# Lightweight convolution into a gated FFN: two of VectorE's 18 convolution group tasks move to GpSimd, and TensorE's convolution blocks become three of 80 windows and one of 40

## The chip, the core and the metric

The kernel runs on one core of one Trainium2 chip. The metric is the device time of one execution in microseconds (us), the median of three runs. The engines are named as the profile names them: PE is TensorE, DVE is VectorE, ACT is ScalarE, POOL is GpSimd, SP is the queue that issues most of the DMAs.

## What is computed

The input `x` is 8 sequences of 3904 rows with 192 channels. Each row becomes a weighted sum of itself and the six rows before it in its sequence (zeros ahead of a sequence's first row). The seven weights are a softmax and are shared by the 24 channels of a head. The result goes through a gated feed-forward network without a nonlinearity. Cut to what matters:

```
w   = softmax(weight, axis=-1)                      # 8 heads x 7 taps
y   = einsum('hk,bskhg->bshg', w, windows(x))       # causal, 7 taps, each sequence by itself
out = ((y @ w1) * (y @ w2) @ w3) @ w_out            # 192 -> 1024 -> 1024 -> 192
```

`w3 @ w_out` is multiplied out once at the start (`W_sb`, 1024 x 192), so that each row costs a first product (192 to 1024, twice), an elementwise product, and a second product (1024 to 192).

## The kernel before

**Rows and rounds.** The 31232 rows are two streams of TS = 15616 rows, which are worked on side by side. A round R is CH = 512 rows of both streams, and there are NR = 31 rounds (the last has 256 rows). Channels are kept on 64 partitions per stream, in NP = 3 groups k of 64 channels.

**Phases.** Rounds 0 to 2 are written out by hand at the start. From round 3 on the work goes in phases of two rounds: phase p has rounds 2p+1 and 2p+2, and there are phases 1 to 14 (phase 0 has second products alone). In the loop at L744 a phase first issues the first products of its two rounds (`first_product`, L497), then four second products of rounds that lie two behind (`second_product`, L531). For each of the eight parts `ft` of a round, PE makes `pa` and `pb` in PSUM (L512), ACT copies `pa` to `asb` (L519), and DVE multiplies `asb` with `pb` into `abT` (L521). All PSUM tiles share one tag with four buffers (L92), so PE can be at most four tiles ahead of the engines that empty them. A second product is 32 matmuls (L537), a copy to SBUF by ACT into `osb` (L542), and an output DMA on SP (L547). `osb` lies in a tag of five buffers (L102).

**The convolution, on PE.** Most rounds get their input from PE. Rows are cut into windows of 32 rows of which 26 are new. A block of windows is loaded by POOL's DMAs with a cast (`x_jobs`, L136), convolved with a 32 x 32 band matrix in 32 x 32 tiles of PE (`conv`, L305; matmuls L323), copied from PSUM (L332), stored to DRAM by SP (`store`, L339), and read back transposed by SP into the ring `xT` (`transposes`, L391). `SIZES` (L49) gives the blocks' numbers of windows. Each block from number 4 on is cut into units of channels (L714): a unit's PSUM tile holds up to 512 columns, so that a block of 40 windows is two units of 96 channels (64 matmuls of 120 columns each), and a block of 80 is four units of 48 channels (32 matmuls of 240 columns each). `places` (L637) says behind which second products of which phase a unit stands: `3: (0,)` is one unit behind the first second product of phase 3.

**The convolution, on DVE.** The phases in `SIDE` (L48) get their input without PE. Their 6 phases x 3 channel groups are the 18 group tasks (L415). For each task POOL's DMA casts x into `rows_c` (`side_cast`, L432), SP transposes it into one of five `raw` buffers (`side_transpose`, L444), ACT makes the first product with a tap (`side_first`, L451), and DVE adds the other six taps (`side_sums`, L458; one instruction a tap at L472, 1024 elements wide, or two where a sequence starts inside the phase). The result goes to one of two `side` tiles, which the SIDE phases use in turn. L640 to L654 hand out these sums: a phase gets 7 of them, or 8 if it is in `places` (`room`, L644), and they stand in DVE's queue behind the phase's `abT` products, beside the second products.

**POOL's pace.** From phase 1 on POOL's DMAs (casts and window loads) are given out at six points of a phase, behind `abT` parts 1, 3, 5, 7 of the first round and 2, 4 of the second (`points`, L728). At each, POOL copies two elements of `abT` (L749), which holds its queue until DVE has come that far, and then issues its DMAs.

## Time and profile before

| | |
|---|---|
| time, median of three runs | 515.36 us (515.12 to 515.78) |
| the profiled execution | 516.07 us |
| its span, first to last instruction | 514.4 us, so 1.67 us lie around it |
| mean granted TensorE clock | 0.999 |
| ACT busy | 353.6 us (69%), 403 instructions |
| POOL busy | 87.7 us (17%), 180 instructions |

The profile is one execution, as the hardware profiler took it. Times count from the span's start. "Busy" is the time in which an engine had an instruction under way, and a group line gives the source line, the engine, the operation, output <- input, the count, and behind the bar the busy time in us, the mean of one in ns, and the idle time ahead of them with what ended it. The chain of waits is followed back from the last instruction to what released each step, so its shares say what the end waited for. A view by stretches gives, for stretches of the span that the reader chooses, each engine's busy time in us, with the number of instructions as (x...).

### The profile page before, as it was taken

To read this page: it belongs to the slowest core of one execution; us is meant where nothing else is said; L and a number is where in the kernel's file an instruction comes from. 1 tells how busy PE (TensorE), PEld (TensorE's weight loads), DVE (VectorE), ACT (ScalarE), POOL (GpSimd) and SP (SyncE) were. 2 spreads that over 40 slices of the span, in tenths; PEclk is the share of its full clock that TensorE was granted. 3 is DMA by queue.
4 is the path that set the end of the run, shared out by engine and by line. 5 is a ranking of instruction groups with operands and counts; after the bars stand their busy time and mean duration, and the time that the engine had idled before them with its cause. 6 is when DMAs were issued, how large, how long until landed. Compare 5 with 4: busy or idle time off the path is not lost.

```text
span 514.4 us, 14129 instructions
## 1 busy us (share of the span) xinstructions
PE 508.4 (99%) x6020; PEld 335.9 (65%) x6020; DVE 446.5 (87%) x430; ACT 353.6 (69%) x403; POOL 87.7 (17%) x180
## 2 busy tenths in 40 slices
PE   8999999999999999999999999999999999999997
PEld 4446856758557585675855748567585675856777
DVE  6798699999899998989989899898998989989880
ACT  6886677677776777757677776675757757576562
POOL 8975031030220302103022030200000000000000
PEclk9999999999999999999999999999999999999999
DMA  9999999795996969937567699834023083210304
GB/s 133 148 167 157 183 122 251 153 127 101 158 172 164 141 88 199 81 124 63 84 95 63 141 187 168 144 32 144 1 64 94 2 197 66 65 62 1 124 3 154
DMA packets 154189, 59.46 MB, mean 116 GB/s; under 512 B 108945, under 2 KB 154125, under 8 KB 154125
## 3 DMA queue, kind: packets, MB, share of 16 engines
q0 software_dynamic: 66912, 17.07, 38.5%
q1 hardware_dynamic: 87053, 41.38, 35.6%
q8 instruction: 47, 0.77, 0.6%
q14 instruction: 17, 0.14, 0.1%
q10 hardware_dynamic: 160, 0.10, 0.1%
HBM read 34.42 MB, written 34.88 MB: 135 GB/s over the span
## 4 chain that ended last, share of the span: by engine, by line
PE 93%; DVE 3%; ACT 1%; DMA 1%; issue 1%; POOL 0%; POOLq 0%
PE pa L512 30%; PE pb L512 30%; PE ops L537 30%; PE cps L323 2%; DVE acc L472 1%; DVE abT L521 1%; PE wps L605 1%; DMA xb<-in_x_dram 1%; ACT asb L519 1%; ACT convo L332 0%; DVE side L472 0%; PE ops L558 0%; PE tps L385 0%; PE tps L370 0%; POOL xb L157 0%
## 5 line engine op out<-in xcount | busy, mean ns | idle before, releaser
L521 DVE TENSOR_TENSOR abT<-asb,pb 128x1024 bf16<-128x1024 bf16 x240 | 292.5, 1221 | 40.8 <-ACT asb L519 25.3
L519 ACT CAST asb<-pa 128x1024 bf16<-128x1024 f32 x244 | 247.0, 1012 | 63.7 <-PE pa L512 63.3
L512 PEld LDWEIGHTS <-wn 64*128 64x128 bf16 x1488 | 138.1, 94 | 83.5 <-issue 2.2
L512 PEld LDWEIGHTS <-ws 64*128 64x128 bf16 x1488 | 130.5, 94 | 71.3 <-issue 1.5
L537 PE MATMUL ops<-W_sb,abT 128*128 128x192 bf16 x1936 | 164.8, 246 | 0.0
L537 PEld LDWEIGHTS <-abT 128*128 128x128 bf16 x1936 | 158.2, 98 | 7.8 <-issue 7.5
L512 PE MATMUL pb<-xT,wn 64*128 64x512 bf16 x456 | 124.0, 376 | 0.0
L512 PE MATMUL pa<-xT,wn 64*128 64x512 bf16 x456 | 123.1, 376 | 0.2
L512 PE MATMUL pa<-xT,ws 64*128 64x512 bf16 x456 | 123.1, 376 | 0.0
L512 PE MATMUL pb<-xT,ws 64*128 64x512 bf16 x456 | 121.7, 376 | 0.0
L542 ACT COPY osb<-ops 128x768 f32<-128x768 f32 (+1 forms) x61 | 48.5, 794 | 84.2 <-PE ops L537 84.2
L472 DVE SCALAR_TENSOR_TENSOR acc<-raw,wC,acc 128x1024 f32<-128x1024 bf16 (+3 forms) x90 | 88.4, 1014 | 1.2
L512 PE MATMUL pb<-side,wn 64*128 64x512 bf16 (+1 forms) x288 | 75.0, 367 | 0.2 <-DVE abT L521 0.2
L512 PE MATMUL pa<-side,wn 64*128 64x512 bf16 (+1 forms) x288 | 74.5, 367 | 0.1
L512 PE MATMUL pa<-side,ws 64*128 64x512 bf16 (+1 forms) x288 | 74.6, 367 | 0.0
L512 PE MATMUL pb<-side,ws 64*128 64x512 bf16 (+1 forms) x288 | 73.6, 367 | 0.0
L749 POOL COPY pace<-abT 1x2 bf16<-1x2 bf16 x48 | 8.4, 174 | 215.0 <-DVE abT L521 215.0
L332 ACT CAST convo<-cps 128x640 bf16<-128x640 f32 (+2 forms) x62 | 34.1, 634 | 2.5 <-PE cps L323 2.4
L157 POOL DMA_DIRECT2D xb<-in_x_dram x46 | 30.3, 662 | 12.8 <-issue 5.8
L438 POOL DMA_DIRECT2D rows_c<-in_x_dram x36 | 27.4, 762 | 9.2 <-issue 8.8
L472 DVE SCALAR_TENSOR_TENSOR acc<-side,wC,acc 128x320 f32<-128x320 bf16 (+13 forms) x30 | 24.9, 879 | 0.3
L472 DVE SCALAR_TENSOR_TENSOR side<-raw,wC,acc 128x1024 bf16<-128x1024 bf16 (+1 forms) x14 | 17.4, 1246 | 0.5
(68 smaller groups left out, 125.1 us busy)
## 6 DMA issues: line engine op xcount, KB each, us to landing
out_dram<-osb SPq DMA_DIRECT2D x58, 384.0 KB
xb<-in_x_dram POOLq DMA_DIRECT2D x28, 240.0 KB, 6.7
rows_c<-in_x_dram POOLq DMA_DIRECT2D x30, 130.0 KB, 4.2
rows<-convo SPq DMA_DIRECT2D x13, 120.0 KB
rows<-convo SPq DMA_DIRECT2D x6, 240.0 KB
xb<-in_x_dram POOLq DMA_DIRECT2D x6, 228.0 KB, 7.7
w3b<-in_moe_w_dram POOLq DMA_DIRECT2D x4, 256.0 KB, 5.3
w3b<-in_moe_w_dram POOLq DMA_DIRECT2D x8, 128.0 KB, 5.4
```

Of the source, the lines that this page charges most:

```text
L157: nc.gpsimd.dma_start(out=tiles[js[0]][0][group(r, e), s:s + w, :], in_=bass.AP(tensor=x.tensor, offset=(r * TS + t - PAD) * D, ap=[[D, C] ...
L323: nc.tensor.matmul(o.rearrange("p (w g) -> p w g", g=wd)[:, :, c - c0:c1 - c0], Aband[group(r, e), h, :], xb[group(r, e), s:s + m, c:c1], ...
L332: f(out=convo[:, e::E, k, :, lo:lo + c] .rearrange("p w r g -> p r w g"), in_=src[:, :, :, o:o + c])
L438: nc.gpsimd.dma_start(out=rows_c[t0 - HALO:t1, k, r * Q:r * Q + Q], in_=x_rows[r * TS + t0 - HALO:r * TS + t1, k * Q:k * Q + Q])
L472: nc.vector.scalar_tensor_tensor(out=side_of[p][:, k, 0:t1 - t0] if last else a, in0=raw[:, HALO + lo - t0 - d:HALO + hi - t0 - d], scalar ...
L512: nc.tensor.matmul(p[:, r, f * N:f * N + N], w_of(i, k, r)[rs, ft * 128:(ft + 1) * 128], operand(R, k, rs), start=(k == 0), stop=(k == NP ...
L519: nc.scalar.copy(out=asb[:, :, 0:per * N], in_=pa[:, :, 0:per * N])
L521: nc.vector.tensor_tensor(out=ab[:, f0, :, 0:N], in0=asb[:, :, 0:N], in1=pb[:, :, 0:N], op=ALU.mult)
L537: nc.tensor.matmul(ops[:, g // 2, (g % 2) * D:(g % 2) * D + D], ab[:, jt, r, g * 128:(g + 1) * 128], W_sb[:, jt, :], start=(jt == 0), stop ...
L542: nc.scalar.copy(out=osb.rearrange("p (a g) d -> p a (g d)", g=2), in_=ops[:, 0:ng // 2, 0:2 * D])
L605: nc.tensor.matmul(wps[:, q, 0:D], w3T[:, g, q, :, :, t].rearrange("p j b -> p (j b)"), wo_b[:, g, t, :], start=(g + t == 0), stop=(g == G ...
L749: P(out=pace, in_=abT_of[R][0:1, ft, 1, 0:2])
```

## The change

`SIDE` becomes phases 3, 6, 7, 10, 11 and 14 instead of 3, 7, 8, 11, 12 and 14, and with that the rounds that PE convolves fall into one block of 40 windows and three of 80 (of 280 windows in all, as before). `places` moves their units. Two of the 18 group tasks, channel group 2 of phases 7 and 11, are taken from ACT and DVE (`BY_POOL`). POOL makes them in four halves of 512 columns: for each half a transpose by SP into a buffer of its own (`pool_transpose`), then seven jobs, one a tap (`pool_sums`): a product of 512 elements, and for all but the first an addition of 512 elements. The jobs stand behind POOL's pace copies, three or four a phase in phases 3 to 10, and always behind that point's DMAs (`pool_at`; three a phase use points 0, 2 and 4, four use 0, 1, 3 and 4). The two tasks' casts and four transposes are still issued, the transposes one half at a time.

For space, `wo_b` moves to a tag that POOL's accumulator takes over, and `osb` gets four buffers instead of five. The output DMAs of rounds 27 and 28 are split in two, as those of 29 were. DVE's sums are handed out 6 to phase 0 instead of 5, and 8 instead of 7 only to phases with two units.

```diff
@@ -45,8 +45,8 @@
     C = 32
     ST = C - PAD
     LAG_ROWS = (LAG + 1) * CH
-    SIDE = (3, 7, 8, 11, 12, 14)
-    SIZES = [20, 20, 20, 40, 40, 80, 40, 80, 40]
+    SIDE = (3, 6, 7, 10, 11, 14)
+    SIZES = [20, 20, 20, 40, 40, 80, 80, 80]
     NB = len(SIZES)
     FIRST = [sum(SIZES[:b]) for b in range(NB)]
     XN = 20 * D
@@ -100,7 +100,7 @@
         return psum.tile([128, 16, 128], BF16, tag="banks", name=name)
 
     def slot(shape, dtype, name):
-        return stage.tile(shape, dtype, tag="slot", bufs=5, name=name)
+        return stage.tile(shape, dtype, tag="slot", bufs=4, name=name)
 
     rows = dram.tile([TS, NP * NS * Q], BF16, name="rows")
     rows_c = dram.tile([TS, NP, NS * Q], BF16, name="rows_c")
@@ -412,7 +412,8 @@
     def side_span(p):
         return (2 * p + 1) * CH, min((2 * p + 3) * CH, TS)
 
-    tasks = [(q, k) for q in SIDE for k in range(NP)]
+    BY_POOL = ((7, 2), (11, 2))
+    tasks = [(q, k) for q in SIDE for k in range(NP) if (q, k) not in BY_POOL]
     side_of, acc_of, raw_of = {}, [], []
     RAW = HALO + 2 * CH
 
@@ -429,8 +430,8 @@
             side_of[q] = (a if i % 2 == 0 else b)[:, 0:NP * 2 * CH].rearrange(
                 "p (k t) -> p k t", k=NP)
 
-    def side_cast(i):
-        p, k = tasks[i]
+    def side_cast(i, task=None):
+        p, k = task or tasks[i]
         t0, t1 = side_span(p)
 
         def job(r):
@@ -476,6 +477,50 @@
             return run
         size = (t1 - t0) / (2 * CH)
         return [(size, job(d, d == 0)) for d in list(range(2, K)) + [0]]
+
+    pool_raw, pool_acc, pool_tmp = [], [], const.tile([128, CH], FP32, name="tmp")
+
+    def pool_tiles():
+        t = stage.tile([128, 3 * CH + HALO], BF16, tag="wo", bufs=1, name="acc")
+        pool_acc.append(t[:, 0:2 * CH].bitcast(FP32))
+        pool_raw.append(t[:, 2 * CH:3 * CH + HALO])
+
+    def pool_half(p, k, half):
+        lo = side_span(p)[0] + half * CH
+        return p, k, lo, [z for z in range(0, TS, S) if lo <= z < lo + CH]
+
+    def pool_transpose(p, k, half):
+        _, _, t0, _ = pool_half(p, k, half)
+        nc.sync.dma_start_transpose(out=pool_raw[0], in_=rows_c[t0 - HALO:t0 + CH, k, :])
+
+    def pool_sums(p, k, half):
+        _, _, t0, starts = pool_half(p, k, half)
+
+        def product(out, d):
+            nc.gpsimd.tensor_scalar(
+                out=out, in0=pool_raw[0][:, HALO - d:HALO - d + CH],
+                scalar1=wC[:, k, K - 1 - d:K - d], scalar2=None, op0=ALU.mult)
+
+        def job(d):
+            def run():
+                acc, tmp = pool_acc[0], pool_tmp
+                if d == 1:
+                    product(acc, 1)
+                    for z in starts:
+                        nc.gpsimd.memset(acc[:, z - t0:z - t0 + 1], 0.0)
+                    return
+                product(tmp, d)
+                if d == 0:
+                    o = half * CH
+                    nc.gpsimd.tensor_tensor(out=side_of[p][:, k, o:o + CH], in0=acc, in1=tmp,
+                                            op=ALU.add)
+                    return
+                for lo, hi in zip([t0] + [z + d for z in starts], starts + [t0 + CH]):
+                    a = acc[:, lo - t0:hi - t0]
+                    nc.gpsimd.tensor_tensor(out=a, in0=a, in1=tmp[:, lo - t0:hi - t0],
+                                            op=ALU.add)
+            return run
+        return [job(d) for d in list(range(1, K)) + [0]]
 
     def operand(R, k, rs):
         if phase_of(R) in side_of:
@@ -541,7 +586,7 @@
         osb = slot([128, ng, D], FP32, "osb")
         nc.scalar.copy(out=osb.rearrange("p (a g) d -> p a (g d)", g=2),
                        in_=ops[:, 0:ng // 2, 0:2 * D])
-        n = ng if R < NR - 2 else ng // 2
+        n = ng if R < NR - 4 else ng // 2
         for g in range(0, ng, n):
             t0 = r * TS + R * CH + g * 128
             (nc.scalar if g and (R, r) == (NR - 1, NS - 2) else nc.sync).dma_start(
@@ -566,7 +611,7 @@
 
     W_sb = const.tile([128, JT, D], BF16)
     GQ = DFF // 4
-    wo_b = const.tile([128, GQ // 64, 2, D], BF16)
+    wo_b = stage.tile([128, GQ // 64, 2, D], BF16, tag="wo", bufs=1, name="wo_b")
     w3b_of, w3T_of = {}, {}
 
     def load_wo():
@@ -634,14 +679,13 @@
     phases = [()] + [(R, R + 1) for R in range(LAG + 1, NR, 2)]
     assert phases[-1][-1] == NR - 1
 
-    places = {0: (0, 1), 1: (2,), 2: (0, 1, 2), 3: (0,), 4: (0,), 6: (0, 2), 7: (0, 2),
-              10: (0,), 11: (0,)}
+    places = {0: (1, 2), 1: (2,), 2: (0, 1, 2), 5: (0, 2), 6: (0, 2), 9: (0, 2), 10: (0, 2)}
     starts, chain, room, p = {}, {}, 0, -1
     for i, (q, k) in enumerate(tasks):
         for cost, f in side_sums(i):
             while room < cost:
                 p += 1
-                room = 5 if p == 0 else 8 if p in places else 7
+                room = 6 if p == 0 else 8 if len(places.get(p, ())) == 2 else 7
                 at, ends = 0, {}
                 starts.setdefault(p, [])
             if not chain or chain[max(chain)][-1][0] != i:
@@ -716,9 +760,16 @@
              for h in range(0, H, n)]
     assert sum(map(len, places.values())) == len(units)
     jobs = {p: [] for p in range(1, len(phases))}
-    for p, b, part in ((1, 5, 1), (2, 6, 0), (4, 7, 0), (5, 7, 1), (8, 8, 0)):
+    for p, b, part in ((1, 5, 1), (3, 6, 0), (4, 6, 1), (7, 7, 0), (8, 7, 1)):
         jobs[p] += x_jobs(b, part)
+    pool_at = {3: 4, 4: 3, 5: 4, 6: 3, 7: 4, 8: 3, 9: 4, 10: 3}
+    halves = [(q, k, h) for q, k in BY_POOL for h in range(2)]
+    pool_sum = [f for v in halves for f in pool_sums(*v)]
+    assert sum(pool_at.values()) == len(pool_sum)
+    pool_from = {2: halves[0], 4: halves[1], 6: halves[2], 8: halves[3]}
     casts = [(p - 1, f) for p in starts if p > 1 for i in starts[p] for f in side_cast(i)]
+    casts += [(p, f) for p, t in zip((2, 6), BY_POOL) for f in side_cast(None, t)]
+    casts.sort(key=lambda c: c[0])
     for p in jobs:
         due_now = sum(d <= p for d, _ in casts)
         ahead = max(due_now, min(len(casts), 6 - len(jobs[p])))
@@ -744,22 +795,31 @@
     for p, rounds in enumerate(phases):
         todo = jobs.pop(p, [])
 
-        def issue(R, ft, n):
+        each = -(-len(todo) // len(points))
+        at = [[todo.pop(0) for _ in range(min(each, len(todo)))] for _ in points]
+        for v in {0: (), 2: (1, 4), 3: (0, 2, 4), 4: (0, 1, 3, 4)}[pool_at.get(p, 0)]:
+            at[v].append(pool_sum.pop(0))
+
+        def issue(R, ft, fs):
             def run():
                 P(out=pace, in_=abT_of[R][0:1, ft, 1, 0:2])
-                for _ in range(min(n, len(todo))):
-                    todo.pop(0)()
+                for f in fs:
+                    f()
             return run
 
-        each = -(-len(todo) // len(points))
         for j, R in enumerate(rounds):
-            first_product(R, {ft: issue(R, ft, each) for a, ft in points if a == j and todo})
+            first_product(R, {ft: issue(R, ft, at[v])
+                              for v, (a, ft) in enumerate(points) if a == j and at[v]})
         assert not todo
         for b in {u[0] for u in units[:3]}:
             for xb, p0, w in zero_rows.pop(b, []):
                 nc.gpsimd.memset(xb[p0:p0 + PAD, w, :], 0.0)
         for i in starts.get(p + 1, ()):
             side_transpose(i)
+        if p == 0:
+            pool_tiles()
+        if p in pool_from:
+            pool_transpose(*pool_from[p])
         state = set()
         last = NR if p == len(phases) - 1 else done + 2
         seconds = [(R, r) for R in range(done, last) for r in range(NS)]
@@ -773,7 +833,7 @@
         for R in due[:2]:
             transposes(R)
         del due[:2]
-    assert not units and not due and not jobs and done == NR and sent[0] == len(conv_rounds)
+    assert not pool_sum and not units and not due and not jobs and done == NR and sent[0] == len(conv_rounds)
 
 
 # ---- launch: one core; inputs and outputs as the reference has them ----
```

## What was predicted

> **What bounds the kernel now.** I read the page's busy shares first, then the chain of waits, then the stretches, one for each phase.
>
> ```profile
> PE 508.4 (99%) x6020; PEld 335.9 (65%) x6020; DVE 446.5 (87%) x430; ACT 353.6 (69%) x403; POOL 87.7 (17%) x180
> PE 93%; DVE 3%; ACT 1%; DMA 1%; issue 1%; POOL 0%; POOLq 0%
> PE pa L512 30%; PE pb L512 30%; PE ops L537 30%; PE cps L323 2%; DVE acc L472 1%; DVE abT L521 1%; PE wps L605 1%; DMA xb<-in_x_dram 1%; ACT asb L519 1%; ACT convo L332 0%; DVE side L472 0%; PE ops L558 0%; PE tps L385 0%; PE tps L370 0%; POOL xb L157 0%
> ```
>
> PE has work in 99% of the span and carries 93% of the chain. DVE at 87% is close, yet holds 3%. So time goes where PE gets less to do or stops waiting; DVE's relief counts only where it now makes PE wait. The phases show both (length, busy time by engine):
>
> ```profile
> 65.55:97.50 31.95, 31.95 (x355) 20.80 (x356) 30.08 (x33) 23.17 (x24) 6.05 (x12) 1.00 1.16 172
> 97.50:130.38 32.88, 32.88 (x419) 21.02 (x420) 30.89 (x34) 25.86 (x31) 5.36 (x12) 1.00 0.77 136
> 130.38:162.64 32.26, 32.26 (x386) 21.21 (x388) 29.46 (x33) 22.25 (x25) 5.66 (x12) 1.00 1.28 161
> 162.64:194.90 32.26, 32.26 (x386) 21.32 (x388) 30.08 (x31) 23.17 (x26) 5.35 (x12) 1.00 0.83 125
> 194.90:226.45 31.55, 31.55 (x322) 21.37 (x324) 28.91 (x24) 20.44 (x21) 6.02 (x14) 1.00 0.89 138
> 226.45:258.87 32.42, 32.42 (x387) 21.13 (x388) 29.25 (x24) 23.97 (x27) 5.69 (x12) 1.00 0.61 87
> 258.87:291.29 32.42, 32.42 (x386) 21.01 (x388) 29.65 (x25) 23.97 (x27) 5.62 (x12) 1.00 0.66 92
> 291.29:323.15 31.86, 31.67 (x322) 20.93 (x324) 28.55 (x24) 21.43 (x22) 5.22 (x12) 1.00 1.20 167
> 323.15:354.65 31.50, 31.50 (x322) 20.88 (x324) 28.36 (x23) 20.39 (x21) 3.49 (x8) 1.00 0.58 98
> 354.65:386.90 32.25, 32.25 (x386) 21.35 (x388) 29.09 (x24) 22.25 (x25) 0.00 (x0) 1.00 0.20 58
> 386.90:419.20 32.30, 32.30 (x387) 21.17 (x388) 29.68 (x25) 22.25 (x26) 0.00 (x0) 1.00 0.29 66
> 419.20:450.89 31.69, 31.63 (x322) 21.70 (x321) 28.81 (x26) 21.04 (x22) 0.00 (x0) 1.00 0.40 104
> 450.89:482.38 31.49, 31.49 (x322) 20.64 (x324) 28.53 (x26) 20.18 (x21) 0.00 (x0) 1.00 0.16 51
> ```
>
> These are phases 1 to 13. Phases 9 and 13 have no convolution unit on PE: 31.50 and 31.49 us, the bare length. Phases 3, 4 and 10 have one unit of a 40-window block: 32.26, 32.26 and 32.25, so such a unit costs 0.76. Phases 6 and 7 have two units of an 80-window block: 32.42, so 0.46 each; phase 1 with one (31.95) and phase 2 with three (32.88) give 0.45 and 0.46. PE's length is a plain sum.
>
> **What it removes on PE.** A block of 40 is two units, 2 x 0.76 = 1.52. A block of 80 is four, 4 x 0.46 = 1.84. Blocks 4 to 8 were 40, 80, 40, 80, 40: 3 x 1.52 + 2 x 1.84 = 8.24. Blocks 4 to 7 become 40, 80, 80, 80: 1.52 + 3 x 1.84 = 7.04. That is **1.20 us** less, with as many columns: 128 matmuls of 120 columns go, and 128 of the rest become twice as long. The two units of block 4 stay in phase 0, each one second product later; they cost there what they did.
>
> **What it removes in waits.** Three phases are longer than the sum, and I looked at why on the chain of waits, on DVE and on POOL:
>
> ```profile
> 303.91 1.23 DVE abT L521
> 305.18 0.82 PE pb L512 x6
> 418.42 1.30 DVE side L472
> 419.72 0.04 issue
> 419.76 0.39 PE pa L512 x2
> 303.91 3.48 DVE L521 TENSOR_TENSOR abT<-asb,pb 128x1024 bf16<-128x1024 bf16 x3 [0.50 <-POOL pace L749]
> ```
>
> Phase 12's input is made by DVE just before it: the last sum ends at 418.42 + 1.30 = 419.72, and only then PE goes on. Phases 11 and 12 together take 63.99 where 32.25 + 31.50 = 63.75 are due: **0.24 us**. After the change phase 12 isn't in SIDE, and no input is that late. In phase 6 the six sums for group 1 of phase 7 come ahead of two sums for phase 10; phase 10 has all six for group 1 of phase 11 first; phase 14's are complete in phase 12. In phase 8, 31.86 against 31.50, DVE starts one product 0.50 late and PE waits. The profile names the pace copy, but the program has this product wait for copies of the phase before, so its true cause is open: **0.36 us** that I take as gone, and that could come back elsewhere. Phase 5 gives 0.05 the same way. Together 0.65.
>
> **What DVE and ACT lose.** Two tasks are 12 sums and two first products:
>
> ```profile
> L472 DVE SCALAR_TENSOR_TENSOR acc<-raw,wC,acc 128x1024 f32<-128x1024 bf16 x40 | 51.3, 1283 | 0.9
> L454 ACT ACTIVATE acc<-raw,wC 128x1024 f32<-128x1024 bf16 x12 | 13.8, 1154 | 0.0
> ```
>
> 12 x 1.283 = 15.4 us of DVE and 2 x 1.154 = 2.3 of ACT lie beside PE: nothing by themselves. What they buy is the order above. DVE's worst phase is 8 sums of which 7 are split at a sequence's start (phase 6, for phase 7 and then phase 10), as phase 3 has now:
>
> ```profile
> 152.78 2.72 DVE L472 SCALAR_TENSOR_TENSOR acc<-raw,wC,acc 128x128 f32<-128x128 bf16 x4
> 157.02 6.42 DVE L472 SCALAR_TENSOR_TENSOR acc<-raw,wC,acc 128x894 f32<-128x894 bf16 x9
> 164.53 20.59 DVE L521 TENSOR_TENSOR abT<-asb,pb 128x1024 bf16<-128x1024 bf16 x16 [1.09 <-ACT asb L519]
> ```
>
> The sums begin 152.78 - 130.38 = 22.4 us into the phase, end at 157.02 + 6.42 = 163.44, and DVE then sits 1.09 idle before its next product. Phase 6 will be 0.92 - 0.76 = 0.16 longer than phase 3, so about 1.2 us are left: no wait. Phase 0's sixth sum, 1.3, starts earlier than now, because no unit's copies stand ahead of ACT's first product any more.
>
> **What POOL gains.** 28 jobs in 8 phases, of which three or four fall in a phase. No row has POOL's operations at this size; the nearest:
>
> ```profile
> L749 POOL COPY pace<-abT 1x2 bf16<-1x2 bf16 x48 | 8.4, 174 | 215.0 <-DVE abT L521 215.0
> L219 POOL COPY ws<-wn 64x256 bf16<-64x256 bf16 x17 | 6.7, 396 | 0.9
> L679 POOL TENSOR_SCALAR taps<-taps,total 8x7 f32<-8x7 f32 x1 | 0.3, 315 | 0.1
> L157 POOL DMA_DIRECT2D xb<-in_x_dram x46 | 30.3, 662 | 12.8 <-issue 5.8
> ```
>
> An element more costs (396 - 174) / 254 = 0.87 ns, so one input of 512 takes 174 + 510 x 0.87 = 0.62 us, the low end of both operations: a job is at least 1.24. If a second input costs as much again, the addition is 174 + 2 x 446 = 1.07, and with 0.14 more for a scalar from memory (315 - 174) the product is 0.76: 1.83. Twice that, 3.7, is my upper end. I take 1.83, the estimate that counts each stream. The last job of a phase stands behind part 2 of the second round, the 11th product of 16, which ends about 1.89 + 11 x 1.29 = 16.1 us into the phase (in phase 4 the sixteen take 20.59, from 164.53 on, and the phase starts at 162.64). With 0.17 of pace and 0.66 of DMA it ends at 18.7, or at 20.6 by the upper end. DVE's sums begin at 22.4. So POOL is through before them, its DMAs come some us later than now with a phase of room, and the results are ready before phases 7 and 11 (last jobs in phases 6 and 10): **0 us**. If that cover went, POOL would run beside L472, which costs PE nothing up to those 1.2 us a phase.
>
> [...]
>
> What runs beside the jobs is the product L521, and POOL's copies at the start show that pair:
>
> ```profile
> 13.82 1.76 POOL L219 COPY ws<-wn 64x256 bf16<-64x256 bf16 x4
> 16.84 2.65 POOL L219 COPY ws<-wn 64x256 bf16<-64x256 bf16 x6
> 13.22 3.64 DVE L521 TENSOR_TENSOR abT<-asb,pb 128x1024 bf16<-128x1024 bf16 x3 [0.24 <-ACT asb L519]
> 17.05 1.22 DVE L521 TENSOR_TENSOR abT<-asb,pb 128x1024 bf16<-128x1024 bf16 x1 [0.18 <-PE cps L323]
> L521 DVE TENSOR_TENSOR abT<-asb,pb 128x1024 bf16<-128x1024 bf16 x240 | 292.5, 1221 | 40.8 <-ACT asb L519 25.3
> ```
>
> Beside the copies a product takes 1.22 us, the mean of all 240: no slowing, though these copies have one input.
>
> **Four osb buffers, split output DMAs.** A buffer comes round after four second products, so within a phase each is new and has a phase to be emptied; at the end the time of four. Four second products, SP's latest output DMA, and the last phase:
>
> ```profile
> 312.48 10.67 PE ops L537 x128
> 304.25 0.40 SPq L547 DMA_DIRECT2D out_dram<-osb  x1
> 500.87 0.80 ACT L542 COPY osb<-ops 128x768 f32<-128x768 f32 x1 [2.38 <-PE ops L537]
> 510.11 0.48 ACT L542 COPY osb<-ops 128x384 f32<-128x384 f32 x1 [0.52 <-PE ops L537]
> ```
>
> The first row is phase 8's four second products. The 304.25 is 13 us into phase 8, and its buffer is written again at that phase's end, 18 us later. At the end the fifth copy (510.11) needs the first's (501.67) DMA done: 8.4 us. I cost both at 0; their bounds are 0 and a microsecond of tail.
>
> **Sum.** 1.20 + 0.65 = 1.85 us. The profiled execution took 516.07; it becomes 514.22. The median of the runs is 0.71 lower, so I forecast 515.36 - 1.85 = **513.5 us**.
>
> **Rivals.**
> - *A new wait eats the gain.* Against the 1.85 stand phase 6's 1.2 us of room, the open 0.36, the 0.24 and late DMAs: phases 3 and 8 have DMA shares of 1.28 and 1.20, and phases 3, 4, 7 and 8 get window loads. If the waits return and 0.6 comes on top, 1.85 - 0.65 - 0.6 = 0.6 is left: 514.8. Chance 0.14.
> - *POOL slows DVE's product.* DVE needs 1.22 us a part where PE needs (31.50 - 10.67) / 16 = 1.30, and has the 1.2 us at a phase's end. The jobs cover 4 x 1.83 = 7.3 us of a phase, so it decides from a slowing of about 1.2 / 7.3 = 16% on. If each excluded the other, phases with four jobs lose 7.3 - 1.2 = 6.1 and those with three 5.5 - 1.2 = 4.3: 4 x 10.4 = 42, or 555 us. Against it stand the copies above. Chance 0.06 for this and milder cases. [...]
> - *The change doesn't do what it says, by gaining on DVE:* if DVE were the bound, 15.4 us would go, 500. PE's 99% speaks against it. Chance 0.01.
>
> **How the numbers follow.** Forecast 0.79, new wait 0.14, slowed product 0.06, DVE-bound 0.01. A measurement of this kernel can tell about 0.2%, 1.0 us. Of the forecast's 0.79, 0.05 may fall short of 1.0; of the new wait's 0.14, 0.04 goes beyond no change. Faster 0.75, same 0.15, slower 0.10. The range goes from 512.9 (0.6 of scatter below, as the three runs of before span 0.66) to 515.6, which takes in the new wait.
>
> **What would show it.** The profile after should have phases of 31.5 with no unit (3, 4, 7, 8, 11 to 13) and 32.42 with two (5, 6, 9, 10); 128 matmuls fewer at the convolution; L521 still at 1.22; POOL's jobs ending before the sums. Wrong it would be if L521 grew, if DVE's idle time ahead of phase 7 were gone, or if PE waited for `side`, `xT` or `xb`.

## The result and the profile after

| | before | after |
|---|---|---|
| median | 515.26 us (515.06 to 516.37, 21 runs) | 514.66 us (513.40 to 515.68, 21 runs) |
| the profiled execution | 516.07, span 514.4 | 514.66, span 513.0 |

The ratio is 0.9983, 95% interval 0.9977 to 0.9990: 0.60 us faster, where 1.85 were forecast. The time lies in the range, the sign is right, and two thirds of the gain are missing. What is also new is the scatter: before, three of 21 executions are more than 0.7 us above the fastest; after, 15 of 21 are, and four are at or below 513.87, near the forecast of 513.5.

The page of the changed kernel, first the engines' busy time, then the chain of waits by engine:

```profile
PE 506.8 (99%) x5892; PEld 332.9 (65%) x5892; DVE 432.4 (84%) x430; ACT 351.6 (69%) x397; POOL 162.8 (32%) x243
PE 97%; DVE 1%; ACT 1%; issue 1%
```

PE has 128 matmuls fewer (6020 to 5892) and carries 97% of the chain, where it was 93%: DVE's 3% are down to 1. The phases 1 to 13 of the changed kernel, in the same columns as before (length, then busy time of PE, PE's weight loads, DVE, ACT, POOL, the granted clock, the DMA share):

```profile
65.96:97.91 31.95, 31.95 (x355) 20.79 (x356) 28.86 (x31) 23.15 (x24) 6.05 (x12) 1.00 1.10 164
97.91:130.79 32.88, 32.88 (x419) 21.09 (x420) 28.59 (x27) 25.82 (x31) 5.67 (x12) 1.00 0.86 134
130.79:162.28 31.49, 31.49 (x322) 20.69 (x324) 28.35 (x23) 20.40 (x21) 15.83 (x23) 1.00 1.11 171
162.28:193.78 31.50, 31.50 (x323) 20.88 (x324) 28.35 (x23) 20.39 (x21) 13.48 (x20) 1.00 0.73 120
193.78:226.20 32.42, 32.42 (x387) 21.10 (x388) 29.40 (x30) 23.97 (x27) 15.65 (x19) 1.00 0.71 95
226.20:258.62 32.42, 32.42 (x386) 21.09 (x388) 29.96 (x33) 25.01 (x28) 14.03 (x18) 1.00 0.61 87
258.62:290.11 31.49, 31.49 (x322) 20.82 (x324) 29.17 (x32) 20.39 (x21) 15.34 (x19) 1.00 1.14 171
290.11:321.61 31.50, 31.50 (x323) 20.73 (x324) 28.76 (x32) 20.40 (x21) 13.23 (x18) 1.00 0.78 121
321.61:354.03 32.42, 32.42 (x386) 21.06 (x388) 29.50 (x27) 23.97 (x27) 15.25 (x19) 1.00 0.63 87
354.03:386.45 32.42, 32.42 (x386) 21.06 (x388) 29.61 (x25) 24.79 (x28) 8.93 (x9) 1.00 0.20 56
386.45:417.95 31.50, 31.50 (x322) 20.74 (x324) 28.32 (x25) 20.18 (x21) 0.00 (x0) 1.00 0.60 130
417.95:449.44 31.49, 31.49 (x322) 20.88 (x324) 26.70 (x24) 20.18 (x21) 0.00 (x0) 1.00 0.30 76
449.44:480.93 31.49, 31.49 (x322) 20.64 (x324) 19.54 (x16) 19.34 (x20) 0.00 (x0) 1.00 0.17 51
```

Every phase has the length that the prediction's working gives it (31.5 without a unit, 32.42 with two units of 80; phases 1 and 2, with one unit and three, are as before), and PE is busy in all of it. Together they take 480.93 - 65.96 = 414.97 us, where before they took 482.38 - 65.55 = 416.83. That is 1.86 less: the whole forecast of 1.85 is there. It was lost ahead of phase 1. One row of the waits of PE from 60 to 70 us, and three of the chain at that place (start, length, what):

```profile
PE ops L582 <- issue: 1.2, 1, 1.2
```

```profile
61.90 2.09 PE ops L582 x24
63.99 1.15 issue
65.14 0.82 PE ops L582 x8
```

In the middle of phase 0's last second product, after 24 of its 32 matmuls, PE stands still for 1.15 us, and the profile shows nothing that it waits for. "Issue" is the name for that.

The two profiled executions also began differently, which has to be taken out before phase 0 can be compared. The chain at the start, before and after:

```profile
2.31 4.90 DMA xb<-in_x_dram
...
9.76 0.91 PE pa L512 x6
```

```profile
8.87 0.91 PE pa L557 x6
```

Before, the first window load came late, and the first product began at 9.76 in place of 8.87. So the profiled execution of before was itself 0.89 late, about what it lies above its median. From the first product to the start of phase 1 it took 65.55 - 9.76 = 55.79, and the changed kernel 65.96 - 8.87 = 57.09. The account of the two executions: -0.89 at the start, +1.30 in phase 0 (1.15 of it idle), -1.86 in phases 1 to 13, +0.05 in the last stretch, together -1.40 of the measured -1.41.

### The profile page after: what moved, and what is told of

It reads as the page before. It is cut to its first block, busy times and chain, and to the rows that moved or that the text cites. A ratio compares the mean times of both kernels' runs of the same rounds, so it can differ in the third digit from the quotient of the medians.

```text
span 513.0 us, 13921 instructions
## 1 busy us (share of the span) xinstructions
PE 506.8 (99%) x5892; PEld 332.9 (65%) x5892; DVE 432.4 (84%) x430; ACT 351.6 (69%) x397; POOL 162.8 (32%) x243
## 4 chain that ended last, share of the span: by engine, by line
PE 97%; DVE 1%; ACT 1%; issue 1%
PE ops L582 32%; PE pa L557 31%; PE pb L557 30%; PE cps L323 2%; PE wps L650 1%; PE warm L233 1%; ACT asb L564 1%; DVE abT L566 0%; ACT convo L332 0%; PE ops L603 0%; PE tps L385 0%; PE tps L370 0%; DVE xT L377 0%; DVE xb L277 0%; DVE Aband L287 0%
## 5 line engine op out<-in xcount | busy, mean ns | idle before, releaser
L566 DVE TENSOR_TENSOR abT<-asb,pb 128x1024 bf16<-128x1024 bf16 x240 | 292.7, 1221 | 56.7 <-ACT asb L564 41.5
L473 DVE SCALAR_TENSOR_TENSOR acc<-raw,wC,acc 128x320 f32<-128x320 bf16 (+4 forms) x90 | 76.2, 894 | 0.7
L805 POOL COPY pace<-abT 1x2 bf16<-1x2 bf16 x55 | 9.6, 175 | 187.0 <-DVE abT L566 186.9
L500 POOL TENSOR_SCALAR tmp<-acc,wC 128x512 f32<-128x512 bf16 x24 | 37.6, 1568 | 0.8
L439 POOL DMA_DIRECT2D rows_c<-in_x_dram x36 | 28.5, 792 | 5.4 <-issue 4.4
L520 POOL TENSOR_TENSOR acc<-acc,tmp 128x512 f32<-128x512 f32 (+6 forms) x25 | 26.0, 1047 | 1.7
```

Source lines behind the costliest of these rows:

```text
L439: nc.gpsimd.dma_start(out=rows_c[t0 - HALO:t1, k, r * Q:r * Q + Q], in_=x_rows[r * TS + t0 - HALO:r * TS + t1, k * Q:k * Q + Q])
L473: nc.vector.scalar_tensor_tensor(out=side_of[p][:, k, 0:t1 - t0] if last else a, in0=raw[:, HALO + lo - t0 - d:HALO + hi - t0 - d], scalar ...
L500: nc.gpsimd.tensor_scalar(out=out, in0=pool_raw[0][:, HALO - d:HALO - d + CH], scalar1=wC[:, k, K - 1 - d:K - d], scalar2=None, op0=ALU.mult)
L520: nc.gpsimd.tensor_tensor(out=a, in0=a, in1=tmp[:, lo - t0:hi - t0], op=ALU.add)
L566: nc.vector.tensor_tensor(out=ab[:, f0, :, 0:N], in0=asb[:, :, 0:N], in1=pb[:, :, 0:N], op=ALU.mult)
```

## The experiments

Each kernel ran beside the kernel before on the same chip. The theory after the result was that the phases are as forecast, and that the missing 1.2 us are PE waiting for its own instructions at the end of phase 0. Its rivals were the sixth part of sums that DVE now has in phase 0, a cost of GpSimd's jobs that the profiled execution hides, and chance.

**again.** The changed kernel, unedited.

> The changed kernel once more, unedited, for a second profile and more times. Theory (the missing 1.2 us of the median are lost ahead of phase 1, where PE runs out of instructions while the DMA engines are full): phases 1 to 13 take 415.0 us again, within 0.2, and what differs from the first profile lies before phase 1's start (65.96 there); median 514.2 to 515.0 with runs over 1.5 us apart. Rival (POOL's jobs or later DMAs cost something in other executions): phases 1 to 13 take 415.5 or more in this profile.

514.49 us (513.27 to 515.40, 11 runs), ratio 0.9982 (0.9972 to 0.9991). The result repeats, and so does its scatter (seven of 11 executions are more than 0.7 above the fastest). In this profiled execution (513.81) PE did not idle: phases 1 to 13 took 414.96, and from the first product to phase 1 it was 55.91. So without the idle time phase 0 costs what it did before (55.79), and the execution is close to the forecast.

**head.** Phase 0 as it was before, all else as changed.

```
-    places = {0: (1, 2), 1: (2,), ...
+    places = {0: (0, 1), 1: (2,), ...
-                room = 6 if p == 0 else ...
+                room = 5 if p == 0 else ...
```

> The changed kernel with phase 0 as it was before: the two units of block 4 behind the first and second of the second products again, and five of VectorE's sums in phase 0 instead of six. Theory (time is lost ahead of phase 1): phase 1 starts at 64.5 to 65.6 us, PE has no idle of over 0.5 us put down to issue, and the median falls by 0.6 to 1.2 against the changed kernel, to 513.4 to 514.1, with less scatter. Rival (lost later, by POOL): median as the changed kernel's, 514.7, with the same scatter.

513.56 us (513.50 to 514.04, 5 runs), ratio 0.9968 (0.9955 to 0.9980): 1.74 us faster than the kernel before beside it (515.30), nearly all that was forecast, and in these five runs the scatter is gone. Phases 1 to 13 take 415.07, and the chain runs into phase 1 without a gap:

```profile
59.92 4.79 PE ops L582 x58
64.70 0.76 PE pa L557 x6
```

This has the lowest median of all that were run, ahead of both kernels. So the change's loss is in the two edits of phase 0: GpSimd's jobs and the blocks are all here.

**units, sums.** The two edits of phase 0 apart. units has the old places and the new six parts of sums; sums the new places and the old five parts.

```
units:  -    places = {0: (1, 2), 1: (2,), ...
        +    places = {0: (0, 1), 1: (2,), ...
sums:   -                room = 6 if p == 0 else ...
        +                room = 5 if p == 0 else ...
```

> The changed kernel with the two units of block 4 back behind the first and second of phase 0's second products, but still six of VectorE's sums in phase 0. Theory (the order of PE's instructions in phase 0 is what costs): PE's next 256 instructions are fetched in time, no idle put down to issue at 62 to 65 us, median 513.4 to 514.0 with runs within 0.7. Rival (the sixth sum costs, not the units): median 514.3 to 514.8 with runs 1.5 us and more apart, as for the changed kernel.

> The changed kernel with five of VectorE's sums in phase 0 instead of six, and the units where the change puts them. Theory (the order of PE's instructions costs): median 514.2 to 514.8, runs 1.5 us and more apart, as for the changed kernel. Rival (the sixth sum costs): median 513.4 to 513.9, runs within 0.7.

units: 513.82 us (513.71 to 513.95, 6 runs), ratio 0.9971 (0.9959 to 0.9982). Steady, and 0.26 above head, which the intervals do not tell apart; but its profile has one wait of PE that head's has not:

```profile
PE pb L557 <- DVE abT L566: 0.3, 1, 0.3
```

In the old order the sixth sum makes DVE late for phase 1, which takes 32.40 in place of 31.95. sums: 513.89 us, but from 513.47 to 517.65 (11 runs), ratio 0.9981 (0.9966 to 0.9997): six runs at 513.5 to 513.9 and five from 514.5 up. So the scatter comes with the units' places and stays without the sixth sum. The median of sums is lower than the theory had it (514.2 to 514.8) and lies where the rival had it; only the scatter speaks for the theory here.

**shift.** If PE waits for instructions that come in blocks, the idle time hangs on the count of instructions ahead of it. 96 PE instructions of the warm-up (48 matmuls into nothing, each with its weight load) are added at the start; the warm-up is cut into smaller matmuls so that it takes about as long.

```
-    warm(6)
+    warm(30, 128)
...
-    warm(2)
+    warm(10, 128)
...
-    warm(4, 256)
+    warm(10, 128)
...
-    warm(2)
+    warm(12, 128)
```

> The changed kernel with 48 more warm-up matmuls of 128 columns at the start (the 512 and 256 wide ones are cut up, about the same time), so that PE's instruction stream is 96 instructions further along everywhere. PE's instructions arrive in blocks of 256 (16 KB). In the changed kernel a block that is asked for in phase 0 at about 58.3 us is needed at 64.0; with 96 more, it is asked for at the start of the first unit (57.9) and needed inside the second (61.6). Theory (PE waits for its instructions): the idle put down to issue moves to about 61.6 us and is longer, 1.3 to 3 us, median 515.3 to 517. Rival (the idle has to do with those second products, their data or the units' place): it stays behind the second unit with 0 to 1.2 us, median within 0.5 of the changed kernel's.

514.91 us (514.49 to 517.52, 11 runs), ratio 0.9996 (0.9984 to 1.0009). PE's waits from 40 to 70 us:

```profile
PE cps L323 <- issue: 0.7, 2, 0.6
PE pa L557 <- DMA xT<-rows: 0.2, 1, 0.2
```

The idle time at 64 us is gone, and two others stand at 48.26 and 62.42, 0.58 and 0.16 long. They are smaller than expected, and the median lies where the rival had it; a second wait shows up, for the transposed rows `xT` that phase 1 begins with. But the count of instructions settles what the times leave open. PE's matmuls and weight loads (the first and second count with x) from the start to the place where it stops, in the changed kernel and then at both places in shift:

```profile
0.00:63.99 63.99, 61.97 (x988) 37.91 (x989) 51.06 (x77) 46.64 (x67) 39.31 (x74) 1.00 1.39 158
...
0.00:62.42 62.42, 60.17 (x988) 39.05 (x989) 48.84 (x74) 44.38 (x63) 39.47 (x74) 1.00 1.35 160
0.00:48.26 48.26, 46.60 (x732) 28.42 (x733) 39.43 (x60) 35.14 (x50) 38.80 (x73) 1.00 1.29 154
```

The changed kernel stops behind 988 matmuls and 989 weight loads, in the last second product. shift stops behind the same count, though that is now another place of the program, inside the second unit; and its first stop is 512 instructions, two blocks of 256, ahead of it. blocks and beside, below, stop behind 988 and 989 too. So what PE waits for hangs on the count, and not on the units or their data.

The block itself can be seen. The changed kernel's page has a queue of its own for instructions (packets, MB, share):

```profile
q8 instruction: 46, 0.75, 0.6%
```

That is 16 KB a packet, and PE's 11784 instructions (5892 matmuls and as many weight loads) divided by 46 are 256. Counted in steps of 256 from the stop's 1977, the moves from 91 us on (37 of the 46) begin between 1.1 us before and 1.1 us behind PE's passing one such place, and end 5.5 to 13.7 us before it comes to the next. The nine before them begin 1.6 to 4.0 us behind it, and the one ahead of the stop is the latest: PE passed 1721 at 58.2, and the move began at 62.3. The DMA queues of the changed kernel from 57 to 62 us, its instruction queue from 62 to 65, and the queues of head from 57 to 62 (packets, MB, share of time; a packet counts whole in the stretch where it starts):

```profile
q1 hardware_dynamic: 974, 0.43, 99.6%
q0 software_dynamic: 894, 0.33, 54.8%
...
q8 instruction: 1, 0.02, 3.3%
```

```profile
q1 hardware_dynamic: 1475, 0.52, 64.9%
q0 software_dynamic: 157, 0.06, 9.3%
q8 instruction: 1, 0.02, 1.2%
```

In head the block came before 62 us (it was moved at 58.2 to 59.1). In the changed kernel none was moved in those five us; it came at 62.3 to 63.8, and PE went on at 65.14, 1.3 us behind its end. In blocks and beside that distance is 1.5. In again the block was there at 62.88 and PE passed the place at 64.29, 1.4 behind it and without stopping: it was just in time. shift's first stop fits as well (a block moved until 47.54, PE on at 48.85); its small one at 62.42 does not, as its block was there at 59.8. Both other queues were busier in the change than in head, but that is no rule: in the same five us sums, without idle time, has q1 at 112.3%, and before has q0 at 76.3%.

**blocks.** The new blocks alone: GpSimd gets no job, DVE keeps 18 tasks.

```
-    BY_POOL = ((7, 2), (11, 2))
+    BY_POOL = ()
...
-                room = 6 if p == 0 else 8 if len(places.get(p, ())) == 2 else 7
+                room = 6 if p == 0 else 9 if p in (5, 6, 9, 10) else 8
...
```

> The new blocks alone: all 18 group tasks stay on ACT and VectorE, with 8 sums a phase and 9 in phases 5, 6, 9 and 10, and GpSimd gets no jobs. Theory (GpSimd buys nothing but VectorE's being in time): PE's units cost what they cost in the changed kernel, but VectorE is late for phase 11 by about 1.8 us (22.4 + 9 x 1.31 = 34.2 us into phase 10, which ends at 32.4) and for phase 7 by 0 to 0.5, so phases 1 to 13 take 416.8 to 417.5 and the time is 516.5 to 517. Rival (VectorE's relief isn't needed): phases 1 to 13 take 415.0 and the time is the changed kernel's or less.

516.17 us (515.17 to 517.38, 11 runs), ratio 1.0011 (1.0002 to 1.0020). PE's 1.20 us are saved here too, yet phases 1 to 13 take 416.77, against 414.97 with the jobs. The chain ahead of phase 11:

```profile
387.33 1.30 DVE side L473
...
388.67 0.39 PE pa L557 x2
```

The phase's input is the work that ends last: PE is through with phase 10 at 387.45 and waits 1.22 for the last sum. This is the wait of phase 12 before, five times as long. So the jobs on GpSimd are what makes the new blocks usable. Whether by the order of DVE's sums or by their number a phase (9 here, 8 with the jobs), this run doesn't tell, since it changes both. The idle time at 64 us is there too (0.95), with no job on GpSimd.

**pool.** GpSimd's jobs alone: blocks, `SIDE`, places and rooms as before.

```
-    SIZES = [20, 20, 20, 40, 40, 80, 80, 80]
+    SIZES = [20, 20, 20, 40, 40, 80, 40, 80, 40]
-    SIDE = (3, 6, 7, 10, 11, 14)
+    SIDE = (3, 7, 8, 11, 12, 14)
-    BY_POOL = ((7, 2), (11, 2))
+    BY_POOL = ((8, 2), (12, 2))
...
```

> GpSimd's jobs alone: blocks, SIDE phases, units and sums a phase as before, with group 2 of phases 8 and 12 made by GpSimd, four osb buffers and the split output DMAs. Theory (relief of VectorE is worth only the wait that it ends): phase 12's wait of 0.24 us goes, phases 1 to 13 take 416.2 to 416.6 us instead of 416.83, and the median is 514.7 to 515.1, with the small scatter of the kernel before, as phase 0 is its own. Rival (GpSimd's jobs cost time): 515.6 or more. Rival (VectorE was the bound): 505 or less.

515.85 us (515.60 to 517.17, 11 runs), ratio 1.0013 (1.0004 to 1.0022). Phases 11, 12 and the last stretch of this version:

```profile
386.52:418.77 32.25, 32.25 (x385) 21.25 (x384) 29.59 (x27) 22.79 (x26) 0.00 (x0) 1.00 0.24 54
418.77:450.32 31.55, 31.55 (x321) 21.50 (x320) 22.97 (x20) 19.39 (x20) 0.00 (x0) 1.00 0.37 98
481.82:514.10 32.28, 29.08 (x353) 22.82 (x352) 15.01 (x13) 16.89 (x19) 0.00 (x0) 1.00 0.26 79
```

Phases 11 and 12 fall from 63.99 to 63.80: the wait of 0.24 is gone, as it should, and phases 1 to 13 take 416.64. Phase 8 is still 31.86 long, so its 0.36 was not DVE's load. But the time is higher by half a us than before, where the rival had it and against my expectation. The last stretch is 0.26 longer than before (32.28 to 32.02), and some 0.4 more lies around the span (516.21 - 514.1 = 2.11, against 1.67). The latter holds for all 11 executions (2.05 to 2.14; 1.67 to 1.83 in the kernel before beside it).

**slots.** To see whether that comes from the edits of space, these alone in the kernel before.

```
-        return stage.tile(shape, dtype, tag="slot", bufs=5, name=name)
+        return stage.tile(shape, dtype, tag="slot", bufs=4, name=name)
-        n = ng if R < NR - 2 else ng // 2
+        n = ng if R < NR - 4 else ng // 2
-    wo_b = const.tile([128, GQ // 64, 2, D], BF16)
+    wo_b = stage.tile([128, GQ // 64, 2, D], BF16, tag="wo", bufs=1, name="wo_b")
```

> The kernel before with only the edits of space: four buffers in place of five for the results, the split of the results' transfers from four rounds before the end in place of two, and the weights' buffer in the pool that is shared. Tells whether the 0.5 us that the version with GpSimd's tasks alone is above the kernel before come from these edits. If they do: 515.6 to 516.0, with the excess after TensorE's last product. If not: 515.1 to 515.4, and it is something in GpSimd's jobs or in how the program begins.

515.89 us (515.46 to 517.43, 11 runs; before 515.55 beside it), ratio 1.0006 (0.9996 to 1.0015). The last stretch is as long as in pool:

```profile
481.62:513.90 32.28, 29.09 (x353) 22.92 (x352) 15.31 (x14) 16.89 (x19) 0.00 (x0) 1.00 0.26 79
```

So those 0.26 us at the end come with the space edits when the blocks are the old ones; with the new blocks the last stretch is 32.07, and the edits cost 0.05. Why they differ is open, and the time of slots is not told apart from that of before. The longer time around the span doesn't come with the space edits: it is 1.66 to 1.80 in slots. It is seen in pool alone, and its cause is open too.

**beside.** The jobs in the place that the change avoids: GpSimd's jobs of a phase stand behind its last product, beside DVE's sums.

```
-            at[v].append(pool_sum.pop(0))
+            late.append(pool_sum.pop(0))
...
+        if late:
+            P(out=pace, in_=abT_of[rounds[1]][0:1, JT - 1, 1, 0:2])
+            for f in late:
+                f()
```

> The changed kernel with GpSimd's three or four jobs of a phase put behind the last product of the phase's second round, so that they run beside VectorE's sums, whose two tensors are both in SBUF, instead of beside the products. Theory (what hides the jobs is where they stand: GpSimd's reads and these sums exclude each other, operation by operation): a sum that meets a job's operation takes up to 1.3 us longer, VectorE loses 3 to 8 us in a phase with jobs and has 1.2 to 1.7 to spare, so phases 3 to 10 grow by 2 to 6 us each, median 530 to 560. Rival (they don't disturb each other): sums at 1.28 us as now, phases 1 to 13 at 415.0 to 415.5, median 514.2 to 515.

535.56 us (535.05 to 535.94, 4 runs), ratio 1.0392 (1.0378 to 1.0406). Groups by form, of the changed kernel and then of beside (count, busy us, mean ns):

```profile
L566 DVE TENSOR_TENSOR abT<-asb,pb 128x1024 bf16<-128x1024 bf16 x240 | 292.7, 1221 | 56.7 <-ACT asb L564 41.5 <-PE cps L323 0.2
L500 POOL TENSOR_SCALAR tmp<-acc,wC 128x512 f32<-128x512 bf16 x24 | 37.6, 1568 | 0.8
L473 DVE SCALAR_TENSOR_TENSOR acc<-raw,wC,acc 128x1024 f32<-128x1024 bf16 x20 | 25.7, 1283 | 0.5
L473 DVE SCALAR_TENSOR_TENSOR acc<-raw,wC,acc 128x128 f32<-128x128 bf16 x10 | 3.4, 345 | 0.0
L520 POOL TENSOR_TENSOR acc<-acc,tmp 128x512 f32<-128x512 f32 x15 | 19.0, 1266 | 1.3
```

```profile
L500 POOL TENSOR_SCALAR tmp<-acc,wC 128x512 f32<-128x512 bf16 x24 | 52.7, 2197 | 1.6
L473 DVE SCALAR_TENSOR_TENSOR acc<-raw,wC,acc 128x1024 f32<-128x1024 bf16 x20 | 33.6, 1679 | 0.5
L473 DVE SCALAR_TENSOR_TENSOR acc<-raw,wC,acc 128x128 f32<-128x128 bf16 x10 | 9.4, 936 | 0.0
```

Beside each other both sides are longer: GpSimd's product goes from 1568 to 2197 ns, DVE's long sum from 1283 to 1679, and the short one of 128 elements from 345 to 936. The short sum loses more than its own length, so this looks like a wait for the other's instruction and not like a share of speed, which no view shows directly. Phases 6 to 10 grow to between 34.25 and 36.99 us, since DVE comes late to the next products; phases 3 and 4, which have jobs too, stay at 31.50 and 31.58, against the expectation. Of the 21 us some 5 are not the jobs' directly: the mean granted clock of beside is 0.990, and 1% of 534 us is 5.3 (an estimate). Beside the product L566, which has one input in PSUM, nothing of the kind is seen: 1221 ns in the change, 1221 before.

**load, unload, best.** What delays the block of instructions? In the change GpSimd's DMAs load windows until 62 us, and SP's transposes for `xT` run from 57.8 on (q0 and q1 above: 54.8% and 99.6% from 57 to 62). load has the old phase 0 and issues the load of block 5's first half twice. unload has the changed phase 0 and issues that load in phase 1; best is unload with the old phase 0.

```
load:            for f in x_jobs(5, 0): f()
                 ->  fs = x_jobs(5, 0);  for f in fs + fs[1:]: f()
unload, best:    for f in x_jobs(5, 0): f()      taken out
                 ((1, 5, 1), (3, 6, 0), ...  ->  ((1, 5, 0), (1, 5, 1), (3, 6, 0), ...
```

> The changed kernel with phase 0 as the kernel before has it, and GpSimd's loads of block 5's first half issued twice in a row (the same rows to the same place, all but the first), so the transfer engines have more to move before 62 us. Theory (load in the transfer engines delays the fetch): the fetch starts at 60 to 62 us in place of 58.2, TensorE idles 0.5 to 1.3 us at 64 us in part of the executions, median 513.9 to 514.8, spread over 1 us. Rival (the order of the units decides, not the load): 513.4 to 513.7 with a small spread, no idle time at 64 us.

> The changed kernel, with one edit: GpSimd's loads of the first half of block 5 are issued in the course of phase 1 and no longer at the end of phase 0's list, so the transfer engines have less to move between 45 and 62 us. Theory: TensorE's idle time at 64 us is a wait for its own instructions, whose 16 KB fetch at 58 to 62 us stands behind loads and transposes in the transfer engines; with fewer loads the fetch starts by about 59 us, the idle time at 64 us is gone in the profile, phases 1 to 13 stay 414.9 to 415.1 us, and the median is 513.4 to 513.9 with a spread below 0.8 us. Rival: it is the order of the conversion units itself, or the transposes alone, that delay the fetch; then the median stays at 514.3 to 514.8 with executions from 513.3 to 515.7. A price of the edit itself would be block 5 late for its first unit in phase 1, 0.3 to 1.5 us of idle time there.

> The changed kernel with phase 0 as the kernel before has it (units of block 4 behind second products 0 and 1, five parts of sums) and the loads of block 5's first half in phase 1. Theory: the idle time is absent already with the old order, so the later loads add nothing: 513.4 to 513.7, as without them. Rival: the old order too loses some tenths to late fetches in part of its executions, then up to 0.2 less, 513.3.

load: 518.38 us (515.26 to 521.21, 12 runs), ratio 1.0045 (1.0020 to 1.0069). PE idles just there, but not for instructions. Its chain:

```profile
59.10 1.26 SPq L395
...
60.41 6.85 DMA xT<-rows
...
67.30 0.39 PE pa L557 x2
```

The block of instructions was moved at 57.7 and was in time. What was late is the third transpose of `xT` for phase 1's first round: issued at 60.4, there at 67.26, while PE wanted it at 65.1. PE waits 2.17. So both the theory and its rival are wrong in what they expected: more load does make the end of phase 0 late, in this profile through `xT` and not through the fetch. The profile is of one of the shorter executions (515.73); what the longer ones wait for is not known.

unload: 520.34 us (519.37 to 521.27, 5 runs), ratio 1.0085 (1.0071 to 1.0100); best: 521.51 us (520.80 to 522.07, 4 runs), ratio 1.0115 (1.0100 to 1.0129). The price of the edit that I had put at 0.3 to 1.5 hides all else: the load comes too late for block 5's unit in phase 1. unload's wait, and the stretch right behind it, with the granted clock as the third figure from the end:

```profile
PE cps L323 <- DMA xb<-in_x_dram: 3.6, 2, 2.1
```

```profile
99.17:102.56 3.39, 3.39 (x23) 3.22 (x22) 0.00 (x0) 1.82 (x2) 0.00 (x0) 0.50 1.19 284
```

PE waits 3.6 us for `xb`, and right behind it the granted clock is 0.50 for 3.4 us. The phase's last second product runs in that stretch. In the chain:

```profile
99.11 4.40 PE ops L582 x32
```

The same 32 matmuls take 2.75 us elsewhere (58.50 to 61.25 in the changed kernel), so the low clock costs 1.65. Phase 1 takes 38.31 in place of 31.95. Of the 6.36 more, 3.6 are the wait and 1.65 the clock; the other 1.1 lie in the unit that waited, while the clock was still 1.00, and are not explained. In load too the executions of 518 us and more have mean granted clocks of 0.993 to 0.997, those below 516.2 of 0.999 to 1.000. unload has no idle time at 64 us, but the changed order without the edit has none in two of its profiles either, so nothing about the fetch is settled by it.

## Why the prediction was right and where it failed

- **PE's units, 1.20 us:** right. All phases have the length that 0.76 and 0.46 a unit give them.
- **The waits, 0.65 us:** right in sum. Phase 12's 0.24 went, by DVE's sums: it returns as 1.22 ahead of phase 11 when GpSimd has no job (blocks) and goes with the jobs alone (pool). The 0.36 of phase 8, whose cause I left open, is not DVE's load: pool keeps it. It went with the new blocks and jobs together (blocks keeps 0.35 there, 31.85). The prediction took it as gone without a cause, so that it came out is luck.
- **Phase 6's room of 1.2 us:** right, no wait; the phase is 32.42.
- **POOL's job:** mis-sized. I took 1.83 us a job; the product is 1.57 and the addition 1.27, so 2.84, between my value and the upper end of 3.7. It had no effect, since the cover was long enough. GpSimd's last job in phase 7, and DVE's sums in the same phase:

```profile
278.10 1.27 POOL L520 TENSOR_TENSOR acc<-acc,tmp 128x512 f32<-128x512 f32 x1
```

```profile
281.02 4.04 DVE L473 SCALAR_TENSOR_TENSOR acc<-raw,wC,acc 128x960 f32<-128x960 bf16 x6
```

  The job ends at 279.37, which is 20.75 us into the phase, just past the 20.6 that went with my upper end; the sums begin 1.65 us later. beside shows what the jobs cost where they do run beside the sums: 21 us, the lower clock with it.
- **The product L521 beside the jobs:** right, 1221 ns before and after.
- **Four `osb` buffers, split DMAs:** 0.05 in the last stretch, against 0; right within its bounds.
- **The step that failed: "The two units of block 4 stay in phase 0, each one second product later; they cost there what they did."** The term was put at nothing, and in the profiled execution phase 0 is 1.30 us longer, 1.15 of it idle. The units do cost what they did when PE's instructions are there (55.91 in again, 55.82 in sums, against 55.79), but in part of the executions PE runs out of them or of `xT` at that place. More than 0.7 us above the fastest of their kind are 27 of 43 executions with the new places (the change, again, sums). With the old ones it is none of 11 in head and units, and 8 of 43 in the kernel before, pool and slots, so the old order isn't free of late executions either. Three of five profiles with the new places and the transfers as in the change have 0.93 to 1.15 us of "issue" at 64 us (the change, blocks, beside; not again and sums). None of those with the old places has it (before, head, units, pool, slots, load, best). Going from the change to head is 0.9 to 1.1 us of median. I had looked at what the units cost PE and at the copies behind them, but not at what else was due at that time.
- **Phase 0's sixth sum:** no wait in the change, as predicted, thanks to the new places; in the old order it costs 0.45 in phase 1 (units). So the two edits of phase 0 belong together. Undoing both has the lowest median, though the intervals of head, units and sums overlap.

That the time lies in the range is in part luck. The range reached up to 515.6 for the rival of a new wait, and the measured 514.66 lies close to that rival's 514.8; but the waits that it names (phases 6, 8 and 12, window loads) didn't come, and the one that did is in phase 0, which it does not name. By the 1.0 us that the prediction takes as the least it can tell, the 0.60 is "same", which had a chance of 0.15 against 0.75 for "faster".

What is shown: where the loss is, which edit brings it, and that PE there waits for a block of instructions in the profiles that have the loss, since it stops at one count of instructions wherever that falls in the program. In the ten profiles without such a stop near 64 us (shift apart) the block was there by 62.9 us, in the three with it only between 63.6 and 63.8. What stays open is why it comes that late. A small part is the order itself. Of the 128 matmuls ahead of the place, eight belong to a second product in the old order and to a unit in the new; PE is through the 128 and their weight loads in 5.96 us in before, and in 5.73 and 5.64 in again and sums, so the next block is due 0.2 to 0.3 us sooner behind the one before. The rest is the time until the move began, and that is not explained: load on the transfer engines didn't delay it in load, and lighter load was not tried in a form that left phase 1 undisturbed. In the executions without a profile the scatter can also come from `xT`, which in shift and load is what PE waits for; nothing here tells the two apart.

## What to carry to other kernels

When a kernel's phases add up to 0.02 us, an error sits in the stretches that the sum does not cover: here the start, where PE depends on transfers, transposes and blocks of instructions that came late in some profiles (the block by 1.15 us in the change, `xT` by 2.17 in load), so a unit that is moved there needs its arrivals checked and not only its work. GpSimd's jobs left VectorE's product with an input in PSUM at 1221 ns, and cost 21 us, the lower clock with it, where they met its sums with both inputs in SBUF: choose what they run beside by such a measurement, and size the cover by the upper end of the estimate, since the last job ended there. And judge an edit by the spread of its runs as well as by their median: that 15 of 21 executions were late, where it had been three, told of the loss before any trace did.

## What the hardware showed that I had not expected

- In the change, blocks and beside PE stood still for 0.93 to 1.15 us in straight code, with no wait that the profile shows, always behind 988 matmuls and 989 weight loads, until 1.3 to 1.5 us after a packet of its instruction queue had been moved (46 packets and 0.75 MB for 11784 instructions: 16 KB and 256 each). In these cases the block took 1.2 to 2.2 us to move; in the changed kernel about half of the 46 blocks took 0.9 to 1.0.
- Behind an idle time of 3.6 us in PE in unload (2.06 and 1.55, with 0.3 of work between) the granted clock was 0.50 for 3.4 us, and the second product in that stretch took 4.40 us in place of 2.75, so the wait cost nearly half as much again; behind 2.17 us idle in load the clock stayed at 1.00.
- GpSimd's product of 512 elements with a scalar from memory, bf16 to fp32, takes 1568 ns, longer than its addition of two fp32 inputs (1266 ns), though it has one input less.
- Where GpSimd's jobs met VectorE's sums, which have both inputs in SBUF, both took longer (beside): a product of GpSimd's 2197 ns in place of 1568, a sum of 1024 elements 1679 in place of 1283, and one of 128 elements 936 in place of 345, which is more than its own length.
